# Ten token tiles of layer 1 transposed by DMA from SP's queue instead of on TensorE, in a two-layer attention and token-mixer kernel

## The chip, the cores and the metric

The kernel runs on one core of one Trainium2 chip, in one launch. The metric is device time in microseconds: 1787.47 us before the change, the median of three runs (1786.66 to 1788.98). A core has TensorE (PE, matmuls into PSUM), VectorE (DVE), ScalarE (ACT), GpSimd (POOL) and SyncE (SP), each with its own in-order instruction stream, and a set of DMA engines. SP here only issues DMAs.

## The reference

One sequence of S = 2048 tokens with D = 640 features, 32 heads of 20, bf16. The same pair of blocks is applied twice, with the same weights:

```python
x = x + _A_ref(_layernorm(x), A_wqkv, A_wo)          # attention over 2048 tokens, softmax, 32 heads
x = x + _B_ref(_layernorm(x), B_w1, B_b1, B_w2, B_b2) # token mixer
# _B_ref: u = gelu(einsum("bsd,sf->bdf", h, w1) + b1)   F = 1536, mixing over tokens
#         y = einsum("bdf,fs->bds", u, w2) + b2, transposed back to tokens x features
```

So the kernel computes attention, mixer, attention, mixer. Most of the work is the softmax's 32 x 2048 x 2048 exponentials in each layer.

## The kernel before

**Layout.** Tokens come in 16 tiles of 128 (`tt` 0 to 15), and four tiles make a token block `tb` of 512. The normalized tokens, `h_bf` (128 tokens x 640 features), must stand with features on partitions before they can be projected; this is the tile `hh`, seen as `hT` (128 x 5 x 2048). Each token tile is transposed in five 128x128 pieces (`NDT = 5`).

**Attention.** The heads form 8 groups `g` of 4. For a group, 128 keys and 512 queries, TensorE computes scores `S` (L643) into PSUM tiles of 3 or 2 banks in turn, ScalarE takes the exponential of each score tile into `P` (L705), and TensorE multiplies by the values (`acc`, L1177). Part of the exponentials is computed on VectorE instead, from a PSUM bank `Dt` (L542, L572, L576, L585, with POOL helping at L602). Before scores there must be keys K and queries Q of the group (`proj_fill`, L1028) and values V (`v_fill`, L1052), made from `hT`.

**The planner.** The instruction order on TensorE, VectorE, ScalarE and POOL is not left to a scheduler. While the kernel is built, a planner keeps clocks for the engines (`pem`, `dvm`, `acm`) with measured costs (`WAVE`, `ACT_US`, `PE_TO_DVE` ...) and writes the instructions in the order in which its clocks say that they can run. Score tiles go first; between them `slot_work` places `acc` matmuls, matmuls of zeros that keep TensorE busy (L695), or a *fill*: a group of matmuls and its evacuation from PSUM, with a priority and a time `ready` before which it isn't placed (`add_fill`, `next_fill`, `fill_step`). A projection's `ready` is passed to it by `after` in `t_fill`, when the four tiles of a token block are in `tready`: it is the `at` of the tile for which `after` was called last. VectorE's share of the exponentials begins when the feed has ended (`feed_ended`, which wants all 16 tiles in `tready` and no open feed fill). SP's order is written by the framework's scheduler.

**The feed of layer 1** (`MixFeed`) is layer 0's mixer: for each token tile two fills `y` (L1531, 12 matmuls each of `uT` with `w2s`) are added to bias and residual into `x2s` (L1514), `x2s` is stored to memory by SP (L1518), then `ln_proc` normalizes it into `h_bf` (L812 to L833, or on ScalarE at L842), and `t_fill` puts the transposes on TensorE and a copy from PSUM to `hT` on VectorE or ScalarE. Tiles 0 to 3 of `y` are computed ahead (`mixer_head`), the others between the score tiles. Loads of `w2s` (768 KB for two tiles, L1637) and `x1in` (320 KB, L1483) stand in SP's queue with the stores. `h_bf` has four buffers, and `out_h` holds the tiles that are written and not yet transposed; `allow_apply` keeps them under four. Layer 0's feed (`TokenFeed`) has the same `t_fill` and `out_h`.

**Semaphores.** SP's DMAs use eight completion semaphores in turn; a DMA waits for the one that used the same semaphore eight DMAs earlier. An instruction that reads what a DMA wrote waits for that DMA's own count.

Of the kernel before, what the change touches and what calls it, by code (L numbers as in the profile page):

```python
# [23 lines left out]
D = 640  # L24
# [3 lines left out]
NDT = D // 128  # L28
# [35 lines left out]
POOL_DMA = 0.9  # L64

HOLD = 3
WARM_WAVES = 18
LOG2E = 1.4426950408889634
LN2 = 0.6931471805599453
# [8 lines left out]
def kernel(  # L78
# [12 lines left out]
    nc = tc.nc  # L91
# [139 lines left out]
    def attention(st, x_in_ap, x_mid, uacc_l, feed, feed_stack):  # L231
# [829 lines left out]
            add_fill(("V", part, tt), prio, mms, evac, 320, ready=ready, after=after, act=0.45, fed=fed, gate=gate)  # L1061

        tready = {}

        def when(g, tb):
            return base[tb] + per_g[tb] * g if g < EG else place[(0, g)] + 4.0 * tb

        def t_fill(tt, h_bf, ready, done):
            tb = tt // 4

            def view(t):
                return t[:, :].bitcast(BF16)[:, 0:D].rearrange("p (a b) -> p a b", a=NDT)
            mms = []
            for dt_ in range(NDT):
                def mm(t, dt_=dt_):
                    pe(nc.tensor.transpose(view(t)[:, dt_, :], h_bf[:, dt_ * 128:(dt_ + 1) * 128], ident[:]))
                    if dt_ == NDT - 1:
                        done()
                mms.append(mm)

            def evac(t, end, eng):
                copy_on(eng, hT[:, :, tt * 128:(tt + 1) * 128], view(t))

            def after(end):
                tready[tt] = at = end + DVE_TO_PE
                v_fill(tt, 0, feed.wv_early, when(0, tb) + tt % 4 - 1, at, fed=True,
                       gate=(lambda: len(tready) >= 4) if tb == 0 else None)
                if all(4 * tb + i in tready for i in range(4)):
                    for g in list(range(EG)) + rest:
                        gate = feed.gate_late if g >= EG else None  # L1090
                        owner = next((qb for qb in EQ if part_at[qb] <= g < part_at[qb] + part_rows), None)
                        if owner is not None:
                            gate = lambda owner=owner: feed.gate_late() and not any(qg[0] == owner for qg in early_left)
                        proj_fill("K", g, tb, when(g, tb) - 4, max(at, cx.w_at.get((0, g), at + 1.0)), gate=gate, fed=g < EG)
                        if tb == 0:
                            proj_fill("Q", g, 0, when(g, 0) - 4, max(at, cx.w_at.get((1, g), at + 1.0)),
                                      gate=feed.gate_late if g >= EG else None, fed=g < EG)
                    if tb in EQ and tb > 0:
                        for g in range(EG):
                            proj_fill("Q", g, tb, base[tb] + 16.0 + 8.0 * g - 4, at, fed=True)  # L1100
                if len(tready) == NT and NQB > 1:
                    enqueue_qproj(1)
            add_fill(("T", tt), when(0, tb) - 6 + 0.1 * (tt % 4), mms, evac, D, ready=ready, after=after, wave=0.1,
                     cells=0.25, cost=0.48, act=0.7, fed=True)

        def next_fill(now):
            held = set()
# [212 lines left out]
    class TokenFeed:  # L1320
        groups = 4
        early_qbs = (0,)
        act_helps = True
        act_free = 0.0
        warm_until = 5.6

# [27 lines left out]
        def begin(self, cx):  # L1354
            cx.open_psum()
            nc.scalar.activation(out=warm_act[:, 0:1], in_=mhalf[:, 0:1], func=ACT.Exp, scale=1.0)
            raw, xin = {}, {}

            def load_w(dst, coff):
                nc.sync.dma_start(out=dst, in_=A_wqkv[:, coff:coff + D // 2].rearrange("(dt p) n -> p dt n", p=128))  # L1360

            def load_raw(i, part):
                raw[(i, part)] = self.wp.tile([128, NDT, D // 2], BF16, name="w_raw")
                load_w(raw[(i, part)][:], (D, 0)[i] + part * (D // 2))

            def load_x(tt):
                xin[tt] = self.xp.tile([128, D], BF16, name="x0in")
                nc.sync.dma_start(out=xin[tt][:], in_=A_x[0, tt * 128:(tt + 1) * 128, :])
            for tt in range(4):
                load_x(tt)  # L1370
            load_raw(0, 0)
            load_raw(1, 0)
            load_w(self.wv[:, 0], 2 * D)
            for tt in range(4, 6):
                load_x(tt)
            load_raw(0, 1)
            load_raw(1, 1)
            load_w(self.wv[:, 1], 2 * D + D // 2)
            landing = {tt: 3.2 + 0.5 * tt for tt in range(4)}
            landing.update({4: 9.5, 5: 10.0})  # L1380
            wpads = (wk_pad, wq_pad)

            def pads(i, part):
                return wpads[i][:].rearrange("p a g (j i) -> p a (g j) i", i=32)[:, :, 16 * part:16 * part + 16, DH:32]
            cx.submit(cx.Proc(0, [(0.46, lambda e, i=i: nc.vector.memset(pads(i, 0), 0.0), 0.0) for i in range(2)], 0.9))

            def zero_values(e):
                nc.scalar.memzero(Vv[:, :, :, DH:VW])
                nc.scalar.memzero(Vv[:, :, 4 * self.groups, 0:32 - VW])
                cx.submit(cx.Proc(2.6, [(0.49, lambda e: nc.vector.memset(Vv[:, :, :, DH:DH + 1], 1.0), 0.0)], e + 5.0))  # L1390
            cx.submit(cx.Proc(1.4, [(1.35, zero_values, -0.06),
                                    (0.2, lambda e: nc.scalar.memzero(Vaug[:, NKT * H * VW:]), -0.06)] +
                              [(1.0, lambda e, i=i: nc.scalar.memzero(pads(i, 1)), -0.06) for i in range(2)],
                              2.1, eng=cx.acm))

            def group_copy(i, g):
                eng = cx.acm if g < self.groups else cx.dvm

                def copied(e):
                    src = raw[(i, g // 4)][:].rearrange("p a (h i) -> p a h i", i=DH)[:, :, 4 * (g % 4):4 * (g % 4) + 4, :]  # L1400
                    dst = wpads[i][:, :, g, :].rearrange("p a (j i) -> p a j i", i=32)[:, :, :, 0:DH]
                    if eng is cx.acm:
                        nc.scalar.copy(out=dst, in_=src)
                    else:
                        nc.vector.tensor_copy(out=dst, in_=src)

                def done(e):
                    cx.w_at[(i, g)] = e + 0.05
                    self.second -= g >= self.groups
                ready = 22.0 if g >= self.groups else 11.0 if g else (6.2, 7.5)[i]  # L1410
                cx.submit(cx.Proc((0 if g == 0 else 1.5) if g < self.groups else 5, [(0.5, copied, 0.0)], ready, eng=eng, after=done))
            for g in range(NG):
                for i in range(2):
                    group_copy(i, g)
            out_h = set()
            h = {}

            def start_tile(tt):
                def dst():
                    h[tt] = self.hp.tile([128, D], BF16, name="h_bf")  # L1420
                    out_h.add(tt)
                    return h[tt][:]

                def after(e):
                    if tt + 6 < NT:
                        load_x(tt + 6)
                        landing[tt + 6] = max(14.0 + 0.5 * (tt - 2), e + 3.0)
                        start_tile(tt + 6)
                    cx.t_fill(tt, h[tt], e + DVE_TO_PE, lambda: out_h.discard(tt))
                cx.ln_proc(xin[tt][:], False, dst, 2.5 + 0.01 * tt, landing[tt], after,  # L1430
                           allow_apply=lambda: len(out_h) < 4, cheap=0.04)
            for tt in range(6):
                start_tile(tt)

    class MixFeed:
        groups = 4
        early_qbs = (0, 1)
        act_helps = True
        act_free = 0.0
        warm_until = 0.0  # L1440

# [30 lines left out]
        def begin(self, cx):  # L1472
            ua_all = cx.KT[:].rearrange("p a s -> p (a s)").bitcast(F32)[:, 0:NF * D].rearrange("p (a d) -> p a d", a=NF)
            ua = [ua_all[:, ft, :] for ft in range(NF)]
            cx.w_at.update({(i, g): 0.0 for i in range(2) for g in range(NG)})
            xin, x2, h, out_h, applied = {}, {}, {}, set(), set()
            self.w2 = {}

            def load_x(tt):
# [14 lines left out]
            def normed(tt):  # L1494
                def dst():
                    h[tt] = self.hp.tile([128, D], BF16, name="h_bf")
                    out_h.add(tt)
                    return h[tt][:]

                def after(e):  # L1500
                    applied.add(tt)
                    cx.t_fill(tt, h[tt], e + DVE_TO_PE, lambda: out_h.discard(tt))
                return dst, after

            def next_w2(sp):
# [11 lines left out]
            def y_done(tt, end):  # L1517
                nc.sync.dma_start(out=self.x_out[tt * 128:(tt + 1) * 128, :], in_=x2[tt][:])  # L1518
                if tt + 3 < NT:
                    load_x(tt + 3)  # L1520
                dst, then = normed(tt)
                cx.ln_proc(x2[tt][:], False, dst, 2.5 + 0.01 * tt, end + DVE_NEXT, then,
                           allow_apply=lambda: len(out_h) < 4, on_act=not cx.s_start)

            def y_fill(tt, half, ready):
                c0, c1 = half * (D // 2), (half + 1) * (D // 2)
# [211 lines left out]
```

## Time and profile before

| | |
|---|---|
| median of three runs | 1787.47 us (1786.66 to 1788.98) |
| the profiled execution | 1791.82 us, of which the span from first to last instruction is 1789.6 us |
| busy in the span: PE, DVE, ACT, POOL | 95%, 86%, 94%, 20% |
| mean granted TensorE clock | 0.993 |
| transposes on TensorE (`h_bf`), both layers | 160 matmuls of about 0.22 us, pipelined |
| transposes of layer 1 | 860.2 to 1026.4 us; those of tiles 4 to 7 from 899 to 904 us |
| score tiles of layer 1 | from 869.9 us on |

The page gives busy time by engine, the chain of work that ended last, and groups of instructions by line. A row of a timeline gives the start, the duration, the engine and line, the tile written and the tile read, the number of merged instructions and, in brackets, the idle time before it and what ended it. "SPq" rows are SP issuing a DMA: their duration is that of the issue and not of the transfer. A row of the table by stage gives a stretch, its length, the busy microseconds of each engine with the number of instructions, the granted TensorE clock as a share of full speed, the DMA engines' busy share and the GB/s.

### The profile page before, as it was taken

What the parts mean: (1) busy time and instruction counts of PE and PEld (TensorE: products, weight loads), DVE (VectorE), ACT (ScalarE), POOL (GpSimd) and SP (SyncE); (2) the same over time, 40 slices, a digit from 0 to 9 for tenths busy, and PEclk for the clock granted to TensorE, in tenths of its full rate; (3) what the DMA queues carried; (4) which work ended last, traced back from release to release, by engine and by line L of the source; (5) the groups of instructions that cost most, each with busy time, mean ns of one, the idle gap of its engine ahead of it and who ended that gap; (6) DMA issues with size and microseconds to landing.
All of it is one profiled execution on the core that took longest, in us unless ns stands there. A gap on an engine that the chain in (4) does not pass through costs nothing.

```text
span 1789.6 us, 42888 instructions
## 1 busy us (share of the span) xinstructions
PE 1702.3 (95%) x17880; PEld 669.4 (37%) x17880; DVE 1542.4 (86%) x2433; ACT 1680.8 (94%) x1508; POOL 360.1 (20%) x539
## 2 busy tenths in 40 slices
PE   8999999999999999999999998999999999999999
PEld 3333333333333344444533432333333333444445
DVE  7479999999999999998543478999999999899972
ACT  8999999999999999997789998999999999899960
POOL 3011111122233121231000011112223331212310
PEclk9999999999999999999999998999999999899999
DMA  4200000011225110057412100001212440101665
GB/s 121 27 1 1 1 2 2 23 51 55 70 53 93 21 46 2 10 88 202 140 50 73 61 1 1 1 2 38 65 49 82 85 73 2 61 2 36 100 212 180
DMA packets 110306, 97.56 MB, mean 55 GB/s; under 512 B 52128, under 2 KB 88608, under 8 KB 110112
## 3 DMA queue, kind: packets, MB, share of 16 engines
q1 hardware_dynamic: 97664, 71.22, 13.2%
q0 software_dynamic: 12448, 23.61, 7.9%
q8 instruction: 139, 2.28, 0.5%
q14 instruction: 55, 0.45, 0.1%
HBM read 55.48 MB, written 39.32 MB: 53 GB/s over the span
## 4 chain that ended last, share of the span: by engine, by line
ACT 48%; PE 24%; issue 21%; DVE 6%; DMA 1%; SPq 0%; POOL 0%; DVEq 0%; ACTq 0%; POOLq 0%
ACT P L705 48%; PE S L643 7%; PE acc L1177 3%; PE misc L921 2%; PE acc L695 2%; PE ya L1615 2%; PE misc L1028 1%; DVE ew L542 1%; DVE et L576 1%; DVE Pd L585 1%; PE um L1602 1%; PE ya L1624 1%; PE yb L1615 1%; DVE ey L572 1%; PE misc L968 0%
## 5 line engine op out<-in xcount | busy, mean ns | idle before, releaser
L705 ACT ACTIVATE P<-S 128x1024 bf16<-128x1024 f32 (+1 forms) x1450 | 1640.2, 1371 | 22.8 <-PE S L643 17.2
L643 PE MATMUL S<-QTq,KT 32*128 32x512 bf16 (+1 forms) x4528 | 589.0, 338 | 67.8 <-ACT P L705 51.2
L602 POOL TENSOR_SCALAR ey<-ew 128x512 f16<-128x512 uint16 x388 | 240.0, 618 | 1012.9 <-DVE et L576 417.7
L643 PEld LDWEIGHTS <-KT 32*128 32x128 bf16 x5144 | 234.4, 91 | 538.7 <-issue 514.2
L1177 PE MATMUL acc<-P,Vaug 128*32 128x512 bf16 (+1 forms) x4504 | 368.4, 346 | 2.5 <-DVE T L733 2.4
L542 DVE TENSOR_SCALAR ew<-Dt 128x512 int32<-128x512 f32 x474 | 323.5, 682 | 21.1 <-PE Dt L643 14.0
L695 PE MATMUL acc<-zr,zw 128*32 128x512 bf16 x4300 | 338.1, 385 | 1.2 <-POOL zr L151 1.2
L585 DVE SCALAR_TENSOR_TENSOR Pd<-ew,et 128x1024 int16<-128x1024 int16 x237 | 297.8, 1256 | 1.0
L576 DVE SCALAR_TENSOR_TENSOR et<-ey,ew 128x1024 f32<-128x1024 f16 x237 | 290.5, 1226 | 2.1
L643 PE MATMUL Dt<-QTq,KT 32*128 32x512 bf16 (+1 forms) x616 | 182.8, 333 | 0.0
L1177 PEld LDWEIGHTS <-Vaug 128*32 128x32 bf16 x5120 | 103.6, 94 | 179.8 <-issue 170.8
L572 DVE TENSOR_TENSOR ey<-ey 128x1024 f16<-128x1024 f16 x237 | 161.3, 681 | 6.1 <-POOL ey L602 1.5
L695 PEld LDWEIGHTS <-zw 128*32 128x32 bf16 x4448 | 112.0, 97 | 103.3 <-issue 59.9
L829 POOL TENSOR_TENSOR rstd<-veps,mhalf 128x1 f32<-128x1 f32 x60 | 51.4, 857 | 262.1 <-DVE veps L827 204.2
L1177 PE MATMUL acc<-Pd,Vaug 128*32 128x512 bf16 (+1 forms) x616 | 94.1, 338 | 0.0
L1028 PE MATMUL misc<-hh,wq_pad 128*128 128x512 bf16 x305 | 88.4, 383 | 0.1
L930 DVE COPY ustg<-misc 128x320 f32<-128x320 f32 x143 | 68.7, 481 | 10.1 <-PE misc L921 7.3
L968 PE MATMUL misc<-wo_pad,attnT 128*128 128x320 bf16 x384 | 73.6, 306 | 2.2 <-DVE xin L980 1.8
L921 PE MATMUL misc<-h2st,w1st 128*128 128x320 bf16 x384 | 74.6, 302 | 0.0
L921 PEld LDWEIGHTS <-w1st 128*128 128x128 bf16 x672 | 52.2, 97 | 58.6 <-issue 45.7
L733 DVE STREAM_TRANSPOSE T<-acc 128x512 f32<-128x512 f32 x79 | 55.9, 708 | 19.1 <-PE acc L1177 18.9
L1028 PE MATMUL misc<-hh,wk_pad 128*128 128x512 bf16 x240 | 70.7, 386 | 0.0
(135 smaller groups left out, 1141.3 us busy)
## 6 DMA issues: line engine op xcount, KB each, us to landing
uacc<-ustg POOLq DMA_DIRECT2D x72, 320.0 KB, 4.4
w2s<-in_B_w_dram SPq DMA_DIRECT2D x16, 768.0 KB
x1in<-xd SPq DMA_DIRECT2D x24, 320.0 KB
w1st<-in_B_w_dram SPq DMA_DIRECT2D x48, 128.0 KB
xd<-x2s SPq DMA_DIRECT2D x16, 320.0 KB
xin<-xd SPq DMA_DIRECT2D x16, 320.0 KB
w1st<-in_B_w_dram SPq DMA_DIRECT2D x24, 192.0 KB
xd<-x1s SPq DMA_DIRECT2D x12, 320.0 KB
```

The lines of the kernel that those rows point to most:

```text
L542: nc.vector.tensor_scalar(out=w[:, slot, :], in0=Dt[:, :], scalar1=127.0 * FIX, scalar2=0.0, op0=ALU.add, op1=ALU.max)
L572: nc.vector.tensor_tensor(out=y, in0=y, in1=y, op=ALU.mult)
L576: nc.vector.scalar_tensor_tensor(out=box["t"][:, 0:512 * k], in0=ve_y.pop(p)[:, 0:512 * k], scalar=MANT_C * MANT_K ** 2, in1=frac, op0=ALU ...
L585: nc.vector.scalar_tensor_tensor(out=bits, in0=whole, scalar=128.0, in1=box["t"][:, 0:512 * k], op0=ALU.mult, op1=ALU.add)
L602: return engine.tensor_scalar(out=out_ap, in0=in_ap, scalar1=MANT_K / FIX, scalar2=-MANT_K * MANT_S, op0=ALU.mult, op1=ALU.add)
L643: pe(nc.tensor.matmul(out_ap[:, c0:c0 + w], lhsT=KT[32 * j:32 * j + 32, g, kt * 128:(kt + 1) * 128], rhs=get_QT(st, qb)[32 * j:32 * j + 32 ...
L695: pe(nc.tensor.matmul(bank[32 * j:32 * j + 32, :], lhsT=zw[:], rhs=zr[:].to_broadcast([128, 4, 128]), start=start, stop=stop, skip_group_c ...
L705: nc.scalar.activation(out=P[:, 0:ncs, :].rearrange("p a b -> p (a b)"), in_=St[:, 0:ncs, :].rearrange("p a b -> p (a b)"), func=ACT.Exp, ...
L921: pe(nc.tensor.matmul(t[:, 0:w], lhsT=w1_of[(p, ft)][:, sti, :], rhs=rows_in[sti][:, c0:c1], start=(sti == 0), stop=(sti == n_in - 1)))
L968: pe(nc.tensor.matmul(t[:, 0:w], lhsT=attnT[g][:, ttl * 128:(ttl + 1) * 128], rhs=wo_pad[:, g, c0:c1], start=(g == 0), stop=(g == NG - 1)))
L1028: pe(nc.tensor.matmul(t[:, :], lhsT=wpad[:, dt_, g, :], rhs=hT[:, dt_, tb * 512:(tb + 1) * 512], start=(dt_ == 0), stop=(dt_ == NDT - 1)))
L1177: pe(nc.tensor.matmul(acc[32 * j:32 * j + 32, a0:a0 + w], lhsT=Vaug[:, (kt * H + hh_) * VW:(kt * H + hh_) * VW + 32], rhs=P[:, slot, c0:c0 ...
```

## The change

In layer 1, tiles 6 to 15 no longer get a transposing fill. Instead five transposing DMAs from SP write `hT` directly from `h_bf`. The planner counts them with a clock of SP's queue, `turn_free`: each takes `DMA_ISSUE` = 1.28 us of the queue, and the tile counts as there `DMA_LAND` = 2.5 us after the last. `done` now gets the time at which a tile leaves `out_h`, for both layers and both ways, so `out_h` becomes a table of times that `allow_apply` compares with VectorE's clock. Layer 0 (`turned_by_dma = ()`) and the first six tiles of layer 1 are transposed on TensorE as before.

```diff
+DMA_ISSUE, DMA_LAND = 1.28, 2.5
...
         tready = {}
+        turn_free = [0.0]
...
                     if dt_ == NDT - 1:
-                        done()
+                        done(pem["t"] + 0.5)
...
-            add_fill(("T", tt), when(0, tb) - 6 + 0.1 * (tt % 4), mms, evac, D, ready=ready, after=after, wave=0.1,
-                     cells=0.25, cost=0.48, act=0.7, fed=True)
+            if tt not in feed.turned_by_dma:
+                add_fill(("T", tt), when(0, tb) - 6 + 0.1 * (tt % 4), mms, evac, D, ready=ready, after=after, wave=0.1,
+                         cells=0.25, cost=0.48, act=0.7, fed=True)
+                return
+            for dt_ in range(NDT):
+                nc.sync.dma_start(out=hT[:, dt_, tt * 128:(tt + 1) * 128], in_=h_bf[:, dt_ * 128:(dt_ + 1) * 128],
+                                  transpose=True)
+            turn_free[0] = max(turn_free[0], ready + 0.2) + NDT * DMA_ISSUE
+            done(turn_free[0] + DMA_LAND)
+            after(turn_free[0] + DMA_LAND)
...
 class TokenFeed:
+        turned_by_dma = ()
...
-            out_h = set()
+            out_h = {}
...
-                    out_h.add(tt)
+                    out_h[tt] = 1e9
...
-                    cx.t_fill(tt, h[tt], e + DVE_TO_PE, lambda: out_h.discard(tt))
+                    cx.t_fill(tt, h[tt], e + DVE_TO_PE, lambda at: out_h.update({tt: at}))
...
-                           allow_apply=lambda: len(out_h) < 4, cheap=0.04)
+                           allow_apply=lambda: sum(at > cx.dvm["t"] for at in out_h.values()) < 4, cheap=0.04)
...
 class MixFeed:
+        turned_by_dma = range(6, NT)
...
```

`MixFeed` gets the same four edits of `out_h` as `TokenFeed`. In the instruction streams, TensorE loses 50 transposes, VectorE ten copies, and SP gains 50 DMAs. Because the planner's clocks move, the order of the rest of layer 1 moves too: TensorE's streams agree up to the 20th score tile of layer 1, the number of zero matmuls goes from 4448 to 4576, and the number of exponentials on ScalarE and on VectorE stays the same.

More of the change, by code (lines that the diff above doesn't have):

```diff
@@ L1475, in begin @@
             cx.w_at.update({(i, g): 0.0 for i in range(2) for g in range(NG)})
-            xin, x2, h, out_h, applied = {}, {}, {}, set(), set()
+            xin, x2, h, out_h, applied = {}, {}, {}, {}, set()
             self.w2 = {}
@@ L1496, in dst @@
                     h[tt] = self.hp.tile([128, D], BF16, name="h_bf")
-                    out_h.add(tt)
+                    out_h[tt] = 1e9
                     return h[tt][:]
@@ L1501, in after @@
                     applied.add(tt)
-                    cx.t_fill(tt, h[tt], e + DVE_TO_PE, lambda: out_h.discard(tt))
+                    cx.t_fill(tt, h[tt], e + DVE_TO_PE, lambda at: out_h.update({tt: at}))
                 return dst, after
@@ L1522, in y_done @@
                 cx.ln_proc(x2[tt][:], False, dst, 2.5 + 0.01 * tt, end + DVE_NEXT, then,
-                           allow_apply=lambda: len(out_h) < 4, on_act=not cx.s_start)
+                           allow_apply=lambda: sum(at > cx.dvm["t"] for at in out_h.values()) < 4, on_act=not cx.s_start)
             def y_fill(tt, half, ready):
```

## The prediction

> **What bounds the kernel now.** I read the page first, then ScalarE's own timeline where layer 1 starts, then VectorE's, SP's and TensorE's rows of the same microseconds, then the table by stage.
>
> ```profile
> PE 1702.3 (95%) x17880; PEld 669.4 (37%) x17880; DVE 1542.4 (86%) x2433; ACT 1680.8 (94%) x1508; POOL 360.1 (20%) x539
> ACT 48%; PE 24%; issue 21%; DVE 6%; DMA 1%; SPq 0%; POOL 0%; DVEq 0%; ACTq 0%; POOLq 0%
> ```
>
> ScalarE (the exponentials, L705) is busy 1680.8 of 1789.6 us and carries the chain. In the order of the changed kernel ScalarE and VectorE together do exactly as many blocks of 512 exponentials as before, split as before (3622 on ScalarE), so ScalarE's work is the same. The time can change only by ScalarE's idle time: where it waits now, and where it will wait.
>
> ```profile
> 869.89 21.84 ACT L705 ACTIVATE P<-S 128x1536 bf16<-128x1536 f32 x19 [0.43 <-PE S L643]
> 900.07 7.38 ACT L705 ACTIVATE P<-S 128x1024 bf16<-128x1024 f32 x7 [8.34 <-PE S L643]
> 908.79 7.38 ACT L705 ACTIVATE P<-S 128x1536 bf16<-128x1536 f32 x7 [1.35 <-PE S L643]
> 917.22 9.14 ACT L705 ACTIVATE P<-S 128x1024 bf16<-128x1024 f32 x8 [1.05 <-PE S L643]
> ```
>
> These are the first score tiles of layer 1 (nineteen, then from the 20th on). ScalarE idles 8.34, 1.35 and 1.05 us for TensorE. After 918 it is full to 1080 (20.00 of 20 us in every stretch from 920 on); the transposes of tiles 8 to 15 lie there, so they hide behind it already.
>
> ```profile
> 896.43 0.61 DVE L833 TENSOR_SCALAR h_bf<-x2s,mv,rstd 128x640 bf16<-128x640 f32 x1 [0.73 <-POOL rstd L829]
> 900.56 0.61 DVE L833 TENSOR_SCALAR h_bf<-x2s,mv,rstd 128x640 bf16<-128x640 f32 x1
> 896.66 0.38 SPq L1637 DMA_DIRECT2D w2s<-in_B_w_dram  x1
> 897.54 0.32 SPq L1518 DMA_DIRECT2D xd<-x2s  x1
> 897.91 0.42 SPq L1483 DMA_DIRECT2D x1in<-xd  x1
> 902.88 0.33 PE L1076 MATMUL misc<-ident,h_bf 128*128 128x128 bf16 x3
> 903.40 0.39 PE L643 MATMUL S<-QTq,KT 32*128 32x512 bf16 x2 [0.19 <-ACT P L705]
> ```
>
> Tiles 6 and 7 are normalized at 897.0 and 901.2; SP issues three loads and stores of 0.32 to 0.42 us between; TensorE transposes tile 7 from 902.9.
>
> ```profile
> 1090.00:1095.00 5.00, 4.38 (x28) 0.85 (x24) 2.87 (x5) 3.48 (x4) 0.62 (x1) 0.50 0.00 0
> 1540.00:1545.00 5.00, 5.00 (x51) 1.97 (x53) 4.74 (x11) 3.45 (x3) 2.06 (x3) 0.52 0.41 131
> ```
>
> The columns are busy us of PE, PEld, DVE, ACT, POOL, then the granted clock. Twice in layer 1 a TensorE wait of 1.2 to 1.8 us is followed by 8 to 15 us at a clock of about 0.5, in which ScalarE starves: 4.6 us of idle at 1080 to 1098, 4.7 us at 1539 to 1551.
>
> **The change part by part.**
>
> *Taken off TensorE and VectorE:* ten tiles of five transposes and one 0.49 us copy. The rows of tiles 6 and 7 cover about 1.3 us of TensorE at 901.9 to 904.0, just before the idle of 1.35 and 1.05 us. In the new order the value and key projections move up by two to three score tiles there, so I take both idles as gone: -2.4 us. For tiles 8 to 15 the gain is nothing, because ScalarE is full beside them (had TensorE been the bound there, 8 tiles x 0.65 us = 5.2 us would be at stake).
>
> *Feed ends sooner:* in the order the first score block for VectorE comes behind score tile 140 of layer 1 where it was 149 (9 tiles of 9.14 / 8 = 1.14 us, 10 us sooner). But VectorE ends with the same number of blocks, so this gives nothing itself. It does reorder the stretch around 1080, whose idle starts with TensorE waiting 1.23 us for VectorE's turn of an accumulator (L733). Whether that comes back can't be read from an order: -4.6 us if gone, 0 if kept; I take half, -2.3.
>
> *Added on SP:* fifty transposing DMAs. No row shows one. Nearest rows from below: SP's other issues, 0.32 to 0.44 us. From above: a DMA of 6 KB (b_t, from POOL) took 4.0 us from issue to landing, were each block to wait for the one before. The diff's planner counts 1.28 us for each and 2.5 us to land. I take these, because the planner's other constants stand on the rows: 0.69 for L542 (682 ns), 0.71 for L733 (708 ns), 1.22 for L585 (1256 ns).
>
> The Trainium skill bears on this (VectorE: DVE Perf Modes, The three transpose paths): it gives the DMA crossbar 1309 ns for a 128x128 bf16 transpose against 390 ns on TensorE, and advises TensorE where PSUM will do. No run here shows the DMA yet; by 1309 ns the sum below would grow by 0.3 us.
>
> *Where the result is awaited:* this decides. The first key projection of the second token block (K g0 tb1) needs tiles 4 to 7. In the planner its due time is that of the tile whose call came last. That is tile 5, still on TensorE; tiles 6 and 7, with later landings, were entered before. So the new order puts K g0 tb1 behind score tile 23 of layer 1, where TensorE arrives before tile 7 can be there. TensorE is in order: behind this matmul stand the score tiles, and behind them ScalarE.
>
> Worked out on the rows: tile 6 is issued from 897.0 for 5 x 1.28 = 6.4 us, to 903.4. Then SP issues w2s, xd and x1in (0.38 + 0.32 + 0.42), to 904.5. Tile 7's five go out from 904.5 to 910.9 and land at 908.3 (first) to 913.4 (last). TensorE reaches K g0 tb1 at about 903.1: behind score tile 23, at 902.49 now, and two value matmuls. The next score tile (903.40 now) follows the first landing, the one after it (904.75 now) the last: 913.4 + 0.3 = 913.7. That is 8.9 us late, and ScalarE, which has one tile in hand, is late by the same: **+8.9 us**. The w2s data (768 KB, 5.2 us from issue to use in the chain at 860) go out ahead of tile 7 and end before its last block, so I add nothing.
>
> *Clock:* about 10 us of TensorE with hardly a matmul is longer than either wait above, so I expect a low clock behind it. Its price from the event at 1540: 1.42 + 0.76 + 1.17 = **+3.4 us** of ScalarE idle.
>
> *Later waits:* for tiles 8 to 13 the order leaves 14 to 22 score tiles (16 us and more) from the last y matmul to first use; y to landing needs 3.7 (tile 7: 897.5 to 901.2, normalization) + 6.4 + 2.5 = 12.6 us. Tiles 14 and 15 have 12 score tiles, 13.7 us: 1.1 us to spare, so 0. Store, loads and w2s behind SP's transposes are due tens of us later: 0. *Layer 0:* TensorE and ScalarE keep their order; three VectorE instructions stand a few places later in the first 30 us: 0, within 1 us.
>
> Sum: -2.4 - 2.3 + 8.9 + 3.4 = +7.6 us. The profiled execution took 1791.82 us (span 1789.6 and 2.2 around it), 4.35 us over the median of 1787.47; I add the difference to the median: **1795 us**.
>
> **Rivals.**
>
> *1, faster: SP issues them like its other DMAs.* At 0.38 us a block tile 6 is out by 899.0, the three others by 900.2, tile 7 by 903.2 and lands at about 906, behind the w2s data (899.0 + 5.2 = 904.2) and the other two: 2 to 3 us of stall, too short for a long spell at low clock. 2.5 - 2.4 - 2.3 = -2.2: 1785, and down to 1783 with the stretch at 1080 cleared. It decides once tile 7 lands before about 907. For it: every SP row. Against: the planner's constant. Chance 0.17. The Trainium skill supports it on another page (Advanced Engine Details and Errata, X-Bar Transpose): it calls transposing DMAs as fast as ordinary ones. No row here can say yet.
>
> *2, much slower: blocks do not overlap, or queue behind w2s.* At twice the planner's time, 2.5 us a block (between 1.28 and the 4.0 of the 6 KB DMA), tile 7 lands at 897.0 + 12.5 + 1.1 + 12.5 + 2.5 = 925.6: a stall of 21 us, and tiles 14 and 15 fall 5 us short as well. +21 + 5 + 3.4 - 4.7 = +25: 1812; midway to the forecast it is 1804. For it: nothing ran crossbar blocks beside w2s. Chance 0.16.
>
> *3, nothing to see: the stall stays, but the stretch at 1080 clears and the clock holds.* 8.9 - 2.4 - 4.6 = +1.9: 1789.4. Chance 0.12, beside 0.53 for the forecast. That the transposes never reach SP is excluded by the order (50 rows); 0.02 is left for a planner whose later part simply runs better.
>
> **How the numbers follow.** A measurement here can tell about 0.2% (3.6 us) from no change. Slower by more: the forecast 0.53 and rival 2 0.16, 0.69 with little outside: 0.70. Same: rival 3 and the upper part of rival 1, 0.17. Faster: the rest of rival 1, 0.13. The forecast alone, with the 1080 stretch kept or gone and the clock term between 0 and twice its size, spans 1789 to 1801. The range leaves out about 0.1 on either side: 1785 to 1806.
>
> **What would show it.** Right: SP rows of about 1.3 us for the transposes; TensorE idle of about 5 and then 5 us at 903 to 914 at L1028, released by the DMA of hh; ScalarE idle of about 9 us there; a clock of about 0.5 to 0.7 in the 5 us behind it. Wrong: SP rows near 0.4 us and no idle over 3 us at L1028 (rival 1); waits at L1052 for tiles 13 to 15 (rival 2); or a second wait at L1028 for tiles 8 to 15, which I hold for covered.

## The result and the profile after

The changed kernel takes **1792.38 us** (median, 1790.99 to 1794.37) where the kernel before, on the same chip, took 1788.37 (1786.24 to 1790.65): ratio **1.0024**, 95% interval 1.0016 to 1.0032, so 4.0 us slower. The profiled execution took 1794.37 us (span 1792.5). That of before, 1791.82 us, lies above all ten executions it is compared with here; this matters below.

The page first: busy time by engine, and the shares of the chain that ended last.

```profile
PE 1700.7 (95%) x17961; PEld 667.1 (37%) x17961; DVE 1541.1 (86%) x2426; ACT 1680.5 (94%) x1507; POOL 355.8 (20%) x534
ACT 50%; issue 22%; PE 19%; DVE 5%; DMA 3%; POOL 1%; SPq 1%; DVEq 0%; ACTq 0%; POOLq 0%
```

No engine's work has moved by more than 5 us: ScalarE is busy 1680.5 us where it was 1680.8. The answer must be in its idle time. Its timeline where layer 1 starts (start, duration, instruction, count, idle before it and what ended it):

```profile
873.10 21.84 ACT L706 ACTIVATE P<-S 128x1536 bf16<-128x1536 f32 x19 [0.43 <-PE S L644]
903.27 4.63 ACT L706 ACTIVATE P<-S 128x1024 bf16<-128x1024 f32 x4 [8.33 <-PE S L644]
916.47 1.02 ACT L706 ACTIVATE P<-S 128x1024 bf16<-128x1024 f32 x1 [8.57 <-PE S L644]
918.84 11.57 ACT L706 ACTIVATE P<-S 128x1536 bf16<-128x1536 f32 x10 [1.34 <-PE S L644]
```

The first idle, 8.33 us, was there before (8.34). The idles of 1.35 and 1.05 us are gone. In their place stand one of **8.57 us**, behind the 23rd exponential, and one of 1.34 us. SP's and TensorE's timelines of the same microseconds say why:

```profile
900.28 6.92 SPq L1110 DMA_TRANSPOSE hh<-h_bf  x5
907.30 0.53 SPq L1649 DMA_DIRECT2D w2s<-in_B_w_dram  x1
907.94 0.66 SPq L1530 DMA_DIRECT2D xd<-x2s  x1
908.65 0.42 SPq L1495 DMA_DIRECT2D x1in<-xd  x1
909.17 6.21 SPq L1110 DMA_TRANSPOSE hh<-h_bf  x5
```

```profile
906.02 0.45 PE L1053 MATMUL Dt<-wv,hh 128*128 128x320 bf16 x2
915.22 0.61 PE L1029 MATMUL misc<-hh,wk_pad 128*128 128x512 bf16 x1 [8.76 <-DMA hh<-h_bf]
915.76 0.61 PE L644 MATMUL S<-QTq,KT 32*128 32x512 bf16 x2
916.30 1.89 PE L1029 MATMUL misc<-hh,wk_pad 128*128 128x512 bf16 x4
```

SP needs 15.1 us (900.28 to 915.38) to issue tile 6, three plain DMAs and tile 7. TensorE comes to K g0 tb1 at 906.5 and stands for 8.76 us at its first matmul; the next score tile is behind it. The other four matmuls do not wait. From the rows by tile, the issue itself (nanoseconds, min/median/max):

```profile
L1110 SPq DMA_TRANSPOSE hh<-h_bf x50: 1100/1226/2341, 900.3 to 1033.2; - x50
...
  DMA hh<-h_bf: 9.4, 3
```

The second line is all the time that instructions on `hh` waited for a transposing DMA: 9.4 us in three waits, 8.76 of it the one above. Tiles 8 to 15 are covered. The table by stage (busy us of PE, PEld, DVE, ACT, POOL, granted clock, DMA share, GB/s):

```profile
910.00:915.00 5.00, 0.00 (x0) 0.00 (x0) 0.00 (x0) 0.00 (x0) 0.00 (x0) 0.50 0.85 266
915.00:920.00 5.00, 4.78 (x22) 1.10 (x23) 0.69 (x1) 2.19 (x2) 0.00 (x0) 0.56 0.03 7
1090.00:1095.00 5.00, 4.61 (x37) 1.48 (x36) 4.80 (x8) 5.00 (x6) 0.62 (x1) 1.00 0.01 2
1540.00:1545.00 5.00, 4.84 (x68) 2.31 (x69) 4.39 (x9) 5.00 (x6) 1.78 (x3) 1.00 0.01 2
```

For five microseconds no engine computes at all while the DMA engines run at 0.85 (the 768 KB of `w2s`, and the 320 KB each of `xd` and `x1in` issued behind it), and the clock falls to 0.50. The two stretches of before near 1080 and 1540, where ScalarE starved, are full.

The two profiles differ ahead of all this too: layer 1's first exponential starts at 873.10 us where it started at 869.89. Of these 3.2 us, 0.5 come from layer 0's end and 2.7 from the step between the layers. There VectorE waits 3.44 us (to 832.46) for the DMA of `uacc`, TensorE stands meanwhile, and the clock is low behind it. The same stretch in the changed kernel, and in the run below with the load of `w2s` put behind tile 7, which differs from it only in where that load stands:

```profile
835.00:840.00 5.00, 4.81 (x36) 2.00 (x40) 4.37 (x12) 0.00 (x0) 1.95 (x3) 0.50 1.04 389
835.00:840.00 5.00, 4.39 (x75) 2.01 (x64) 3.90 (x12) 0.00 (x0) 1.41 (x2) 1.00 1.06 343
```

In that run layer 1's first exponential starts at 869.18. So these 2.7 us vary between executions and, as far as these profiles tell, are not the change's: over the thirteen profiles the step, from layer 0's last exponential to layer 1's first, takes 38.8 to 42.4 us, and the changed kernel's profile has the longest.

### The profile page after: what moved, and what is told of

The parts are those of the page before. It is cut to its first block, busy times and chain, and to the rows that moved or that the text cites. A ratio compares the mean times of both kernels' runs of the same rounds, so it can differ in the third digit from the quotient of the medians.

```text
span 1792.5 us, 43124 instructions
## 1 busy us (share of the span) xinstructions
PE 1700.7 (95%) x17961; PEld 667.1 (37%) x17961; DVE 1541.1 (86%) x2426; ACT 1680.5 (94%) x1507; POOL 355.8 (20%) x534
## 4 chain that ended last, share of the span: by engine, by line
ACT 50%; issue 22%; PE 19%; DVE 5%; DMA 3%; POOL 1%; SPq 1%; DVEq 0%; ACTq 0%; POOLq 0%
ACT P L706 50%; PE S L644 5%; PE ya L1627 2%; PE acc L1187 2%; PE misc L922 2%; PE acc L696 2%; PE misc L1029 1%; DMA ua<-uacc 1%; DVE et L577 1%; DVE ew L543 1%; DVE Pd L586 1%; PE Dt L1543 1%; PE misc L1543 1%; PE yb L1627 1%; POOL rstd L830 1%
## 5 line engine op out<-in xcount | busy, mean ns | idle before, releaser
L603 POOL TENSOR_SCALAR ey<-ew 128x512 f16<-128x512 uint16 x383 | 235.9, 616 | 1021.2 <-DVE et L577 398.3
L696 PE MATMUL acc<-zr,zw 128*32 128x512 bf16 x4432 | 346.5, 385 | 1.2 <-POOL zr L152 1.2
```

Of the source, the lines that this page charges most:

```text
L603: return engine.tensor_scalar(out=out_ap, in0=in_ap, scalar1=MANT_K / FIX, scalar2=-MANT_K * MANT_S, op0=ALU.mult, op1=ALU.add)
L696: pe(nc.tensor.matmul(bank[32 * j:32 * j + 32, :], lhsT=zw[:], rhs=zr[:].to_broadcast([128, 4, 128]), start=start, stop=stop, skip_group_c ...
```

## The experiments

Each was timed in five rounds against the kernel before, in four sets; before's median was 1787.25, 1787.66, 1788.27 and 1788.06 us in them, so kernels of different sets are compared by their ratios. "Attention" is layer 1 from its first exponential to ScalarE's next table load; "tail" is from there to the span's end.

| kernel | us | ratio (95%) | attention | tail | ScalarE blocks |
|---|---|---|---|---|---|
| before | 1788.37 | 1 | 846.9 | 72.8 | 3622 |
| changed | 1792.38 | 1.0024 (1.0016 to 1.0032) | 846.1 | 73.3 | 3622 |
| bookkeeping alone | 1787.76 | 1.0007 (0.9999 to 1.0016) | 843.2 | 71.9 | 3622 |
| tiles 6 and 7 only | 1791.83 | 1.0033 (1.0020 to 1.0045) | 845.7 | 73.8 | 3624 |
| tiles 7 to 15 | 1785.55 | 0.9984 (0.9974 to 0.9993) | 841.2 | 73.4 | 3620 |
| tiles 8 to 15 | 1782.35 | 0.9971 (0.9960 to 0.9981) | 836.7 | 73.2 | 3620 |
| tiles 8 to 15, order moved | 1782.44 | 0.9963 (0.9950 to 0.9975) | 837.6 | 73.8 | 3620 |
| tiles 12 to 15 | 1786.13 | 0.9993 (0.9984 to 1.0001) | 838.3 | 75.1 | 3624 |
| due time mended | 1787.18 | 0.9995 (0.9986 to 1.0004) | 839.4 | 76.6 | 3612 |
| w2s behind tile 7 | 1791.54 | 1.0021 (1.0012 to 1.0030) | 845.8 | 73.0 | 3622 |
| tile 7 from ScalarE's queue | 1793.97 | 1.0032 (1.0021 to 1.0043) | 847.3 | 74.0 | 3622 |
| order only, first | 1786.77 | 0.9997 (0.9988 to 1.0005) | 838.2 | 75.5 | 3624 |
| order only, second | 1784.60 | 0.9975 (0.9965 to 0.9985) | 838.5 | 74.1 | 3624 |

A block of 512 exponentials costs ScalarE 0.453 us (1640.2 us for 3622 in before).

**The due time of K g0 tb1.**

```diff
+                    at = max(tready[4 * tb + i] for i in range(4))
```

> Edit: in after(), the due time of a token block's projections is the latest landing of its four tiles, not that of the tile entered last. In its order K g0 tb1 stands behind the 26th score tile of layer 1 instead of the 23rd, behind the y matmuls of tiles 8 and 9; VectorE takes 484 score blocks instead of 474, ScalarE 3612 instead of 3622. Theory (the loss is the time until tile 7 has landed, whatever stands in the order): without keys there are no scores, so ScalarE still idles 8 to 9 us there, but TensorE is not idle, the clock stays up, and 10 blocks less at 0.453 us bring 4.5 us: 1786 to 1788, about 2 us under before. Rival (the wrong due time alone is the loss): the idle of 8.6 + 1.3 us goes as well, 1778 to 1780.

TensorE no longer waits for a DMA of `hh` anywhere, yet ScalarE idles almost as long. Its timeline:

```profile
915.59 20.45 ACT L706 ACTIVATE P<-S 128x1536 bf16<-128x1536 f32 x18 [8.64 <-PE S L644]
```

With the projection due later, the planner put the end of one fill of `y`, three more and a value projection (905.5 to 913.2), and then K g0 tb1, in one row ahead of the next score tile. The work filled the stall but did not end it: SP issued tile 7 from 905.78 to 911.98, and K g0 tb1 ran from 913.06 to 914.3, about when the last block came in (1.2 us behind its issue in two runs below). ScalarE lost 8.64 us where the changed kernel lost 9.91 and before 2.40. The rest of the gain is VectorE's ten more blocks (484 rows against 474, 4.5 us less for ScalarE), and the tail gave 3.3 us back.

**Only tiles 8 to 15.**

```diff
-        turned_by_dma = range(6, NT)
+        turned_by_dma = range(8, NT)
```

> Edit: only tiles 8 to 15 of layer 1 are transposed by DMA, tiles 6 and 7 by TensorE. Theory: no wait of more than 1 us for the DMA of hh, ScalarE's idle at the 20th to 40th score tile as before (1.35 and 1.05 us), two blocks less on ScalarE (0.9 us): 1 us under before, and up to 5 us under if the two stretches at a low clock stay away. Rival (forty transposes on SP's queue cost by themselves, by contention or later waits): 3 to 4 us over before, as with all ten.

```profile
909.98 7.38 ACT L706 ACTIVATE P<-S 128x1536 bf16<-128x1536 f32 x7 [1.35 <-PE S L644]
```

Forty transposing DMAs remain, of the same price (median 1230 ns), and the idles at 900 to 919 are those of before, 8.33, 1.35 and 1.06 us. No instruction waits for one of the forty. Against the changed kernel the time falls by 0.0053 of 1788, 9.5 us; 7.5 of it are ScalarE's idle in this place (2.41 against 9.91) and 0.9 the two blocks fewer. So these DMAs as such cost nothing that the profile shows; the first two tiles do.

**Only tiles 6 and 7.**

```diff
-        turned_by_dma = range(6, NT)
+        turned_by_dma = (6, 7)
```

> Edit: only tiles 6 and 7 of layer 1 by DMA, tiles 8 to 15 on TensorE. Theory: the whole wait is there (about 8.6 + 1.3 us of ScalarE idle at the 24th and 25th score tile, less the 2.4 us of before), and two blocks more on ScalarE (0.9 us): 4 us over before like the full change, up to 9 over if the stretches at a low clock stay. Rival (the loss is spread over all fifty transposes): a fifth of it, under 1 us over before.

```profile
913.60 1.02 ACT L706 ACTIVATE P<-S 128x1024 bf16<-128x1024 f32 x1 [8.51 <-PE S L644]
915.96 19.58 ACT L706 ACTIVATE P<-S 128x1536 bf16<-128x1536 f32 x17 [1.34 <-PE S L644]
```

The same two idles, and the same loss: ten DMAs do what fifty did. These two runs settle where the time goes.

**Tiles 7 to 15.**

```diff
-        turned_by_dma = range(6, NT)
+        turned_by_dma = range(7, NT)
```

> Only tiles 7 to 15 of layer 1 by DMA: tile 6 goes back to TensorE, and K g0 tb1 stands where the changed kernel has it, behind the same value matmuls. ScalarE does 3620 blocks, as in the kernels with tiles 8 to 15 by DMA (1782.4). Theory (TensorE's wait is SP's queue, one block of 1.23 us after another, counted from tile 6's normalization in the changed kernel and from tile 7's here): tile 7 goes out from about 901 to 907.5 and is usable by 909.5 to 910.5; TensorE comes there at about 904, so it idles 5 to 6 us in place of 8.8, and ScalarE 4.5 to 6.5 in all beyond the first idle of 8.3 in place of 9.9. Less the two idles of before (2.4) that is 2 to 4 us over the kernels from tile 8 on: 1784.5 to 1787, 5 to 8 us under the changed kernel. Rival (it is the single late tile whatever the queue did before it, w2s or a fixed latency): a wait of 8 to 9 us as before, 1788 to 1790.

SP's issue of tile 7 (to 909.04) and TensorE's rows of K g0 tb1, now with one tile in SP's queue:

```profile
901.96 7.08 SPq L1110 DMA_TRANSPOSE hh<-h_bf  x5
...
905.48 0.39 PE L1029 MATMUL Dt<-hh,wk_pad 128*128 128x512 bf16 x1 [0.42 <-DMA hh<-h_bf]
906.36 0.38 PE L1029 MATMUL Dt<-hh,wk_pad 128*128 128x512 bf16 x1 [0.49 <-DMA hh<-h_bf]
...
907.86 0.39 PE L1029 MATMUL Dt<-hh,wk_pad 128*128 128x512 bf16 x1
909.00 0.38 PE L1029 MATMUL Dt<-hh,wk_pad 128*128 128x512 bf16 x1 [0.75 <-DMA hh<-h_bf]
910.23 0.58 PE L1029 MATMUL Dt<-hh,wk_pad 128*128 128x512 bf16 x1 [0.86 <-DMA hh<-h_bf]
```

One reads the blocks arriving one by one, the last two 1.23 us apart, the last 1.2 us behind the end of its issue. Between them TensorE can place a score tile. ScalarE idles 0.80 + 3.69 + 1.21 + 1.05 = 6.75 us beyond its first idle, against 9.91 with two tiles in the queue and 2.41 with none. TensorE's waits came out shorter than the 5 to 6 us expected, 2.5 in all: it reached the projection at 905.1 instead of 904, and other matmuls stand between the waits. ScalarE's loss (6.75 against 4.5 to 6.5) is a little over what the theory gave, and the time is inside its range.

**The load of `w2s` put behind tile 7.**

```diff
+                turn = nc.sync.dma_start(out=hT[:, dt_, tt * 128:(tt + 1) * 128], in_=h_bf[:, dt_ * 128:(dt_ + 1) * 128],
+                                         transpose=True)
+                if tt == 7 and dt_ == NDT - 1:
+                    tc.chain_iter_dep("sp_order", turn.ins)
...
+                    if tt == 7:
+                        self.w2[5] = w2_load(self.w2p, 5, chained=True)
```

> The changed kernel, with the load of w2s (768 KB) that stood ahead of tile 7's five transposing DMAs in SP's queue put behind the completion of the last of them; TensorE's, VectorE's and ScalarE's orders are those of the changed kernel. Theory (the wait of 8.76 us on tile 7's first block is mostly the block standing behind the data of w2s in the DMA engines): tile 7 is issued from 907.3 instead of 909.2, its first block is usable about 2.5 to 3 us after issue (910 to 911, before: 915.2), then TensorE waits again for the last block, issued to about 914, usable at about 915 or sooner; ScalarE's idle of 8.57 us falls to 5 to 7.5, in two parts, and the time by 1 to 3 us under the changed kernel's, 1789 to 1791. Rival (issue and landing of the blocks alone set the wait, whatever stands ahead): the idle falls by the 0.5 us of the load's issue at most, TensorE's first wait stays over 7 us, 1791 to 1792. A third: the late w2s is missed by the y matmuls of tiles 10 and 11: a new wait on w2s of over 1 us and no gain.

```profile
904.86 6.19 SPq L1110 DMA_TRANSPOSE hh<-h_bf  x5
...
907.88 0.61 PE L1029 MATMUL misc<-hh,wk_pad 128*128 128x512 bf16 x1 [5.34 <-DMA hh<-h_bf]
...
910.96 0.59 PE L1029 MATMUL misc<-hh,wk_pad 128*128 128x512 bf16 x1 [0.71 <-DMA hh<-h_bf]
912.21 0.59 PE L1029 MATMUL misc<-hh,wk_pad 128*128 128x512 bf16 x1 [0.66 <-DMA hh<-h_bf]
```

Half a hit. Tile 7's first block, issued from 904.86, was usable 3.0 us later; in the changed kernel, behind the data of `w2s`, 6.05 us (909.17 to 915.22). So the load does hold the first block up. But the last block then sets the end: ScalarE idles 5.15 + 3.29 + 1.24 = 9.68 us where it was 9.91, and the time is the same within the intervals and the one that the rival gave. The expected 5 to 7.5 us overlooked that ScalarE needs the score tiles behind the last matmul of K g0 tb1 too, and that these matmuls run at a clock of 0.50 (905 to 915) whether the wait is one or three.

**Tile 7 from ScalarE's queue.**

```diff
+                queue = nc.scalar if tt == 7 else nc.sync
+                queue.dma_start(out=hT[:, dt_, tt * 128:(tt + 1) * 128], in_=h_bf[:, dt_ * 128:(dt_ + 1) * 128],
+                                transpose=True)
```

> The changed kernel, with tile 7's five transposing DMAs issued from ScalarE's queue (behind the 20th exponential) instead of SP's; TensorE's and VectorE's orders are as in the changed kernel. Theory (the wait is set by the rate of one queue: ten blocks of 1.2 us and three loads and stores one after another, 15.1 us from tile 6's first block to tile 7's last): tile 7 goes out beside tile 6, about 905 to 911 instead of 909.2 to 915.4, and TensorE's wait ends about 3 to 4 us sooner. ScalarE spends about 6 us on the issues in which it could do three exponentials, so its idle and issue together are 6.5 to 8 us where its idle was 9.9: 1 to 3 us under the changed kernel, 1789.5 to 1791.5. Rival (the DMA engines do transposed blocks one at a time, whichever queue they come from): tile 7's last block is not usable before about 915, ScalarE loses 9 us or more, 1792 to 1794.

```profile
904.97 6.39 ACTq L1111 DMA_TRANSPOSE hh<-h_bf  x5
911.47 4.85 ACT L706 ACTIVATE P<-S 128x1536 bf16<-128x1536 f32 x4 [10.48 <-DMA hh<-h_bf]
```

This run does not decide between the two. `h_bf` was ready at 901.07, but the issue began only at 904.97, 1.2 us after SP had issued tile 6's last block. In the built order ScalarE's first transposing DMA carries waits for tile 6's DMAs from SP (the profile does not name them), so the two tiles went one after the other by program, and whether they could go side by side was not measured. The exponentials stood behind it for 10.48 us. The number is the rival's, its mechanism was not tested.

**Bookkeeping alone.**

```diff
-        turned_by_dma = range(6, NT)
+        turned_by_dma = ()
```

> Edit: no tile by DMA (turned_by_dma = () in layer 1 too), so only the bookkeeping of out_h is left; TensorE, ScalarE and POOL have the order of before, VectorE has three instructions of layer 0 a few places later. Theory: same as before within 1 us. Rival (the profile of the changed kernel shows layer 0 ending 0.5 us later and the step to layer 1 2.7 us longer, and this comes from the bookkeeping): 3 us over before.

TensorE, ScalarE and GpSimd run in exactly the order of before, and so this is also a second profile of that order. The rows near 1080:

```profile
1082.52 3.28 ACT L706 ACTIVATE P<-S 128x1024 bf16<-128x1024 f32 x3 [1.04 <-PE acc L1187]
1086.75 3.81 ACT L706 ACTIVATE P<-S 128x1536 bf16<-128x1536 f32 x3 [0.94 <-PE Dt L644]
...
1093.45 4.75 ACT L706 ACTIVATE P<-S 128x1536 bf16<-128x1536 f32 x4 [1.29 <-PE acc L1187]
```

The stretch at 1080 is there again (4.45 us of idle in all); at 1540 only 1.2 us are lost where before's profile lost 4.7. So the first belongs to the order, the second came and went.

**Order only, and fewer tiles.** What do the kernels with tiles 8 to 15 gain over *before*? The first order-only kernel undoes the whole change; a second kernel keeps tiles 12 to 15 by DMA (`range(12, NT)`):

```diff
-                    backlog(now) > CFG["VE_BACKLOG"]):
+                    backlog(now) > CFG["VE_BACKLOG"] - (0.5 if layer == 1 and t < 190 else 0.0)):
```

> Undoes the whole change and moves only the order: no tile of layer 1 goes by DMA, and VectorE's share is admitted half a microsecond of backlog earlier for the first 190 slots of layer 1, which moves the turns of the accumulators around 1080 us. VectorE does 472 blocks (before: 474), so ScalarE does two more (2 x 0.453 = +0.9 us). Theory (what the kernel with tiles 8 to 15 by DMA gained came from the cleared low-clock stretch at 1080 alone, and the transposes taken off TensorE give nothing): -4.6 + 0.9 = -3.7 us, 1783.5 beside 1787.2, no ScalarE idle between 1075 and 1100 and the three idles of 8.3, 1.35 and 1.05 us at 900 to 918 as before. Rival (the gain needs the transposes off TensorE): +0.9 us, 1788, within 0.1% of before, even if the stretch at 1080 is gone.

> Only tiles 12 to 15 of layer 1 by DMA (twenty instead of fifty transposes), six more tiles on TensorE than the changed kernel. VectorE 472 blocks (two more for ScalarE, +0.9 us). Theory (the number of transposes taken off TensorE from tile 8 on is worth nothing, any order that clears the stretch at 1080 is worth 4.6 us): the idles at 900 to 918 as before, -4.6 + 0.9 + 0.5 for the bookkeeping = -3.2 us, 1784; if the stretch at 1080 is there in this order, +1, 1788. Rival (each tile taken off TensorE is worth 0.65 us, so that eight of them made the 5 us of the kernel with tiles 8 to 15): -2.6 + 0.9 + 0.5 = -1.2 us, 1786.

Both stretches went, and the attention was 8.7 us shorter than in before's profile. The time was not: the tail was 2.7 us longer in the first and 2.3 in the second, and before's profiled execution had taken 3.5 us more than its median. The theory's 1783.5 and 1784 were too low. In the tail, mixer matmuls on `w1st` still have to run; in TensorE's order the first order-only kernel has 24 of them behind its last scores, the kernel with tiles 8 to 15 has 18, before 6. By tile, the 18 of the first order-only kernel that start after ScalarE's last exponential (1707.7):

```profile
L921 PE MATMUL S<-hh,w1st x12: 299/299/299, 1708.9 to 1710.4; 128*128 128x320 bf16 x12
...
L921 PE MATMUL Dt<-hh,w1st x6: 299/299/309, 1708.1 to 1708.8; 128*128 128x320 bf16 x6
```

An order with 9 of them was tried next (0.75 in place of 0.5 in the diff), and the same edit on top of tiles 8 to 15:

> Again the kernel before with its order moved and no transposing DMA in layer 1: VectorE's share is admitted 0.75 us of backlog earlier in the first 190 slots of layer 1. ScalarE does two blocks more than before (3624 of 512), as in the first order-only kernel (1786.77), but only 9 matmuls of the mixer (w1st) stand behind the last scores where that one had 24. Theory (what such kernels gain in the attention is partly given back in the tail, which was 75.5 us with 24 such matmuls behind the scores and 73.2 with 18): tail 72.5 to 74, attention about 838 us, 1784 to 1785. Rival (the tail does not depend on that order; only taking transposes off TensorE gains): 1786.5 to 1787.5, tail over 75.

> Tiles 8 to 15 by DMA as in the fastest kernel so far (1782.35), with the order of layer 1 moved as in the order-only kernel of this call (0.75 us of backlog, 190 slots): 3620 blocks on ScalarE as there, 13 mixer matmuls behind the last scores instead of 18. Theory (no wait on a transposing DMA, no low-clock stretch, two blocks fewer than before on ScalarE, a tail no longer than 73 us): 1781 to 1783. Rival (the gain of the first such kernel was one order's luck): 1785 to 1788.

The second order-only kernel gains 3.7 us over before (medians; 4.5 by the ratio) with no transposing DMA in layer 1. It is 2.2 us under the first (medians; 3.9 by the ratios of the two sets), and the profiles show 1.4 of that in the tail, 74.1 against 75.5. The count of matmuls alone does not rank the tails (18 gave 73.2, 9 gave 74.1), so what sets them is only partly found; the three kernels with 24 (these two, and the one with the due time mended) have the three longest tails, 75.1 to 76.6, and all others lie from 71.9 to 74.1. The kernel with tiles 8 to 15 repeats its gain in another order. Side by side, 1784.60 and 1782.44 differ by 2.16 us, and ScalarE's four blocks fewer are 4 x 0.453 = 1.81 of it. That leaves 0.35 us for eight tiles of transposes taken off TensorE, less than the intervals of the two ratios can tell from nothing. The profiles agree: the 10.2 us of attention between before and the first kernel with tiles 8 to 15 are the two stretches (4.6 + 4.7) and two blocks (0.9). The two kernels with tiles 8 to 15 by DMA are the fastest of all, at 1782.4 us.

## Why the prediction was right, and where its sum was not

*ScalarE's work is unchanged: right* (1680.5 against 1680.8 us). *The first idles gone, -2.4: right*, both rows are gone.

*The wait, +8.9: right in size* (8.57 on ScalarE, 8.76 on TensorE) and in its cause, the queue in front of tile 7, with tile 6 in it. Price and place were read well: 1.28 us a block against a measured median of 1.226. The Trainium skill's 1309 ns (VectorE: DVE Perf Modes, The three transpose paths) lies 7% above the row. Its other sentence, that transposing DMAs are as fast as ordinary ones (Advanced Engine Details and Errata, X-Bar Transpose), does not hold for the time that one takes of SP's queue in these traces, 0.32 to 0.66 us for the plain issues beside the transposes. With it falls rival 1, whose stall of 2 to 3 us was also called too short for a long spell at low clock: with tiles 7 to 15, three waits of 0.42 to 0.75 us within 4 us were followed by a clock of 0.50 from 909.3 to 916.1. What came out otherwise is the shape: not 5 and then 5 us, but one wait at the first block. The step that failed is that the `w2s` data "go out ahead of tile 7 and end before its last block, so I add nothing". They hold up the first block (3.0 us of landing without them, 6.05 with them), and since the last block ends at about the same time either way, the sum was still right: ScalarE lost 9.68 us in all without that load and 9.91 with it. That the one wait at the first block has the size forecast for the last is in part luck.

*The clock, +3.4: mis-sized.* The clock did fall to 0.50 and 0.56, but behind the wait ScalarE lost only 1.34 us, and not all of that need be the clock's: before had an idle of 1.35 us behind the same projection at full clock. The price was taken from the single event at 1540, where the clock was low for 10.2 us (1540.2 to 1550.4) and TensorE was at work in all of them. Here it was low for as long (909.1 to 919.2), but TensorE had matmuls only from 915.22, so 4.0 us of it counted. By that share the price would be 3.35 x 4.0 / 10.2 = 1.3 us, an estimate from these rows that no run tests.

*The stretch at 1080, -2.3: mis-sized by the hedge.* It was 4.6 or nothing, and it went: it was absent from the profiles of all kernels with another order and there in the one with the same.

With these, 7.6 - 0.33 - 2.06 - 2.3 = +2.9 us, where +4.0 was measured. The 1.1 us left are not assigned; the bookkeeping's +0.5 us (medians; by the interval of its ratio -0.2 to +2.9) may be part. Row by row the two profiles cannot be compared for it: the attention in them is even 0.8 us shorter after the change (846.1 against 846.9), because before's profiled execution held 4.6 + 4.7 us of low-clock stretches and took 3.5 us more than its median, and the changed kernel's took 2.0 more than its own, with the long step between the layers. A better partner is the profile of the bookkeeping alone, which has the order of before and took 1788.35 us. Against it the changed kernel's attention is 3.0 us longer (846.1 against 843.2), as the mended sum has it, and its tail 1.3 (73.3 against 71.9); these are single profiles. The prediction allowed for before's profile rightly, by adding its difference to the median.

*Later waits 0: right* (two more waits, 0.6 us in all). *Layer 0 within 1 us: right* (its last exponential ends at 830.74, before 830.24). *Tiles 8 to 15 gain nothing on TensorE: right* as far as the pair above can tell (0.35 us). *The feed ends sooner and gives nothing: right here* (474 VectorE rows in both), but only because the count did not move; with tiles 8 to 15 it is 476, and ScalarE saves the blocks. *Rival 2* had one half of its mechanism, the first block behind `w2s`, but not its price: a block took 1.23 us of the queue and not 2.5. *Rival 3* (1789.4) was right in two of its three parts, stall kept and 1080 cleared, but the clock did not hold; the result lies midway between it and the forecast.

## What to carry to other kernels

Before moving work to a DMA queue, ask for each tile when its first reader stands in the order and what the queue issues between: forty of the fifty transposes were free, the ten of the first two tiles cost ScalarE 7.5 us of idle, and leaving these two on TensorE turned a ratio of 1.0024 into 0.9971. A change of order alone can move a kernel by as much as the change under study (3.7 us here, medians), so a gain is credited to the change only against a kernel that has the new order without it. When a stage ends sooner, look at what it leaves behind for the next: the tail gave back 2.3 to 3.8 us in three kernels.

## What the runs showed of the hardware

- A transposing DMA of a 128x128 bf16 block holds the issuing queue for 1.23 us (median of 50 in the changed kernel, from 1.10 to 2.34), two to four times a plain issue beside it (0.32 to 0.66), and from ScalarE's queue 1.26. The last block of a tile is usable 1.2 us after the end of its issue (with tiles 7 to 15, and with `w2s` behind tile 7).
- A 768 KB load issued 1.9 us ahead of a transposed block on the same queue doubled that block's time to use, from 3.0 (without it) to 6.05 us.
- A TensorE wait of 8.76 us (906.5 to 915.2) took the clock to 0.50 from 909.1 to 919.2, so 6 us of the low clock fell into the wait itself; ScalarE lost 1.34 us behind it. Three waits of 0.42 to 0.75 us within 4 us (tiles 7 to 15) were followed by 0.50 too, for 6.8 us.
- The same order differs between executions: before took 1785.2 to 1792.9 us, the slowest at a mean clock of 0.992 to 0.993.
